# Attention and MLP kernel: batch 2 loaded six tokens to a partition, against odd batches that keep their first 64 tokens for the shared tile

## The chip, the cores and the metric

The kernel runs on one core of one Trainium2 chip. The metric is device time in microseconds (us), the median over runs of the whole program. Engines are named as in the profile: PE (TensorE) multiplies matrices, DVE is VectorE, ACT is ScalarE, POOL is GpSimd, SP is SyncE. POOL, SP and ACT can also issue DMAs.

## The reference, cut to what matters

```python
def _attn_ref(q, k, v, g_norm):                       # 8 batches, 8 heads, 576 tokens, 64 wide
    kv = np.einsum('bhsd,bhse->bhde', k, v)
    out = np.einsum('bhsd,bhde->bhse', q, kv)
    rms = np.sqrt(np.mean(out * out, axis=-1, keepdims=True) + 1e-06)
    return out / rms * g_norm

def _moe_ref(x, g_ln, w_ch1, w_ch2):                  # x: 8 x 576 x 512, heads side by side
    mu = np.mean(x, axis=-1, keepdims=True)
    var = np.mean((x - mu) ** 2, axis=-1, keepdims=True)
    xn = (x - mu) / np.sqrt(var + 1e-06) * g_ln
    ch = np.maximum(xn @ w_ch1, 0.0) @ w_ch2          # 512 -> 2048 -> 512
    return x + ch
```

Attention is linear: for each batch and head a 64 x 64 product of k and v over all tokens, which the queries are then multiplied by. Inputs and output are float32; the matrix products run in bf16.

## The kernel before

The 8 x 576 = 4608 rows of the output are 36 tiles of 128 rows (`TILES`, L81). A batch has 576 = 4 x 128 + 64 tokens: four tiles of its own, and a half. The halves of batches b and b+1 (b even) make one shared tile: tile 8 belongs to batches 0 and 1, 17 to 2 and 3, 26 to 4 and 5, 35, the last, to 6 and 7. Four tiles are a block of the MLP.

**Loads.** All input loads are DMAs issued by POOL, which cast float32 to bf16. POOL's queue is in order and holds eight DMAs at a time: the ninth waits for the first to land. Main loads of a batch put 4 neighbouring tokens on each of 128 partitions (slots 0 to 3); the remaining 64 tokens are loaded apart as a fifth slot (`load_fifth`, L269) on half of the partitions, and the other half of the slot is set to zero. Batches 0 and 1 load k and v with 6 tokens on each of 96 partitions (`load_kv`, L251), 96 x 6 = 576, so that they need no fifth slot; their queries have one as all do. `most` and `rest` (L64, L67) say which 64 tokens go apart: in even batches the last, in odd batches the first. So the rows of a shared tile, the end of one batch and the start of the next, are neighbours in the output and leave in one store (`tile_rows`, L76).

**One batch** (`plan_batch`, L727). For batches 0 to 2 ScalarE (for batch 0 VectorE) copies k from the landing buffer `kb` into `kp` with the heads innermost (`k_permute`, L411), and the queries from `qb` into `qp` (`q_permute`, L417); from batch 3 on the loads write that order themselves (`load_slots`, L282). `kv_mm` (L463) multiplies k by v on TensorE, heads in pairs: 24 matmuls over 96 rows for batches 0 and 1, 20 over 128 rows for the others. VectorE copies the result into `kv_pack` (L479). SP turns the queries with one DMA transpose for a batch (L449; batches 0 and 1 partly on TensorE, L427). From batch 3 on, POOL waits before each group of loads (`gate`, `gate_turn`) until a given earlier tile has been turned, or the queries of the batch before.

**One tile** (`plan_tile`, L822): output matmuls `out_ps` (L491), square on ScalarE (L517), sums (L526) and scaling on VectorE, centring (L579), then the turn of the centred tile into `xT`, on TensorE for the first 12 tiles (L586) with a copy by ScalarE (L593), by an SP DMA afterwards (L597).

**The MLP** (`plan_group`, L927). Up-projection: the first two blocks tile by tile, four groups of 16 matmuls each (`m1_fine`, L636), the others for a block at once (L651). ScalarE evicts each group with a ReLU (L643, L658). Down-projection: 16 matmuls a tile in four groups (L670); VectorE adds the residual (`y_out`, L677), and `store` (L681) writes the tile. Stores are issued by SP, except that the last tile is cut in three parts of 256, 128 and 128 columns, and the middle one is issued by ACT. Up- and down-projection groups share four PSUM banks (`BANKS["mm"]`).

**What sets the order.** Each step is entered with engine, estimated times, key and dependencies (`add`, L104). `run_plan` (L114) simulates the engines, picks for each the ready step with the lowest key within a short horizon, and the steps are emitted in the order of planned starts. Every engine then runs its instructions in that order. A step's `lag` makes the planner count its DMAs as later than estimated. So a changed load also moves matmuls and copies that it does not touch.

Of the kernel before, what the change touches and what calls it, by code (L numbers as in the profile page):

```python
# [14 lines left out]
def kernel(  # L15
# [11 lines left out]
    nc = tc.nc  # L27
# [6 lines left out]
    B, H, S, D = q.shape  # L34
# [15 lines left out]
    NEAR = 0.35  # L50
    BANKS = {"mm": 4, "out": 2, "kvt": 2}
    WARM_FROM = 1.3
    HALVED = (0,)
    SCALED = (0, 1)
    SPLIT_STORE = ()
    HALF_TURN = (0, 1)
    PARTS = ((0, 4), (4, 8))

# [1 line left out]

    def most(b):  # L64
        return slice(64 * (b % 2), 64 * (b % 2) + 512)

    def rest(b):  # L67
        return slice(0, 64) if b % 2 else slice(512, 576)

    def fifth(b):  # L70
        return slice(0, 64) if b % 2 == 0 else slice(64, 128)

    def no_fifth(b):
        return fifth(b + 1)

    def tile_rows(bs, t):  # L76

        return (bs[0] * S + most(bs[0]).start + t, 4) if t < 4 else (bs[0] * S + 512, 1)


    TILES = []  # L81
# [162 lines left out]
    kv_pack = [consts.tile([128, HP, 128], bf16, name=f"kv_pack{i}") for i in range(3)]  # L244

    def kv_view(buf, b):
        if b < 2:
            return buf[b % 2][0:96, :].rearrange("p (h t d) -> p h t d", h=H, t=6)
        return buf[b % 2][:, 0:H * 4 * D].rearrange("p (h t d) -> p h t d", h=H, t=4)

    def load_kv(buf, src, b, h0=0, h1=H):  # L251
        t = 6 if b < 2 else 4
        n = 576 if b < 2 else 512
        tokens = slice(0, 576) if b < 2 else most(b)
        def fn():
            nc.gpsimd.dma_start(  # L256
                kv_view(buf, b)[:, h0:h1, :, :].rearrange("p h t d -> p h (t d)"),
                src[b, h0:h1, tokens, :].rearrange("h (p t) d -> p h (t d)", t=t))
        return fn, n * (h1 - h0) * 256

    def load_q(b, t0, t1):
        def fn():
            nc.gpsimd.dma_start(
                qb[:, :, t0:t1, :].rearrange("p h t d -> p h (t d)"),
                q[b, :, most(b), :].rearrange("h (p t) d -> p h t d", t=4)[:, :, t0:t1, :]
                .rearrange("p h t d -> p h (t d)"))
        return fn, 128 * H * (t1 - t0) * 256

    def load_fifth(dst, src, b):  # L269
        def fn():  # L270
            nc.gpsimd.dma_start(
                dst[fifth(b), :, :], src[b, :, rest(b), :].rearrange("h p d -> p h d"))
        return fn, 64 * H * 256

    def load_slot(dst, src, b, t, h0=0, h1=H):
        def fn():
            nc.gpsimd.dma_start(  # L277
                dst[:, t, h0:h1, :],
                src[b, h0:h1, most(b), :].rearrange("h (p t) d -> p t h d", t=4)[:, t, :, :])
        return fn, 128 * (h1 - h0) * 256  # L280

    def load_slots(dst, src, b):  # L282
        def fn():
            nc.gpsimd.dma_start(
                dst[:, 0:4, :, :],
                src[b, :, most(b), :].rearrange("h (p t) d -> p t h d", t=4))
        return fn, 128 * H * 4 * 256


# [172 lines left out]

    def kv_mm(b, hps):  # L463
        ps = psum.tile([128, HP, 128], f32, tag="kvt", name="kv_ps", bufs=BANKS["kvt"])
        p, last = (slice(0, 96), 5) if b < 2 else (slice(0, 128), 4)
        for hp in hps:
            for t in range(last + 1):
                nc.tensor.matmul(  # L468
                    ps[:, hp, :],
                    lhsT=kp[b % 2][p, t, 2 * hp:2 * hp + 2, :].rearrange("p h d -> p (h d)"),  # L470
                    rhs=(v5[b % 2][:, 2 * hp:2 * hp + 2, :] if b >= 2 and t == 4
                         else kv_view(vb, b)[:, 2 * hp:2 * hp + 2, t, :]),
                    start=(t == 0), stop=(t == last))
            att[b]["kv", hp] = ps
# [203 lines left out]
            x[:, f0:f1], in0=st[n]["m2ps", f0], scalar=blk[m]["rstd"][:, i, :],  # L678
            in1=x[:, f0:f1], op0=ALU.mult, op1=ALU.add)

    def store(n, eng, f0=0, f1=Dm):  # L681
        r0, step = tile_rows(*TILES[n])
        eng.dma_start(out_flat[r0:r0 + 127 * step + 1:step, f0:f1], st[n]["x"][:, f0:f1])


    k0p = []
# [40 lines left out]
    def plan_batch(b):  # L727
# [23 lines left out]
        else:  # L751
# [9 lines left out]
                    pool_do(0.1, lambda: nc.gpsimd.tensor_copy(  # L761
                        mark, att[b - 1]["qT"][:, 0, 0:1]), [adone[b - 1]["qfree"]])
            dk = [adone[b - 2]["kvmm"]]
            if b < 4:

                pool_do(0.5, lambda: nc.gpsimd.memset(kp[b % 2][no_fifth(b), 4, :, :], 0.0), dk)
            gate(f - 8 if b > 3 else 5)
# [2 lines left out]
            if by_slot:  # L770
                pool_load(("k", b), load_slots(kp[b % 2], k, b), rate1, dk)
            else:
                pool_load(("k", b), load_kv(kb, k, b), rate4, dk)
            pool_load(("k", b), load_fifth(kp[b % 2][:, 4, :, :], k, b), 180.0, dk)
            def some_q():
                gate(f - 7 if b > 3 else 6)
                if by_slot:
# [24 lines left out]
            for t in range(5):  # L802
# [6 lines left out]
        s = add("PE", 1.12 if b > 1 else 1.34, 1.35 if b > 1 else 1.57, (p - 17.5 if b == 1 else ok - 4), vdeps + kperm,  # L809
                lambda: kv_mm(b, range(HP)), alloc="kvt")  # L810
        a = add("DVE", 0.34, 0.38, (p - 17 if b == 1 else ok - 2), [s, z1[4], z1[5]] + outs_before,
                lambda: kv_out(b, 0, HP, nc.vector, False))
# [114 lines left out]
    def plan_group(i, kind, a, c):  # L927
        if kind == "m1f":
            g = add("PE", 0.89, 1.1, i, done[a]["xT"] + load["w", 1, c], lambda: m1_fine(a, c),
                    alloc="mm", main=True)  # L930
            g.frees = add("ACT", *act_cost(512), i + 1, [g], lambda: m1_fine_out(a, c))
            done[a].setdefault("m1", []).append(g.frees)
            blk[a // 4]["m1done"] = g
        elif kind == "m1":
            g = add("PE", 0.864, 1.1, i, [d for j in range(4) for d in done[4 * a + j]["xT"]], lambda: m1_block(a, c),
                    alloc="mm", main=True)
            g.frees = add("ACT", *act_cost(512), i + 1, [g], lambda: m1_block_out(a, c))
            blk[a].setdefault("m1outs", []).append(g.frees)
            blk[a]["m1done"] = g
        else:  # L940
            n, m = a, a // 4
            m1s = done[n]["m1"] if m in FINE else blk[m]["m1outs"]
            split = n == N_TILES - 1
            parts = ((0, 256), (256, 384), (384, 512))
            if split:

                if c:
                    return
                for f0, f1 in parts:
                    w = (f1 - f0) / 256  # L950
# [12 lines left out]
            g = add("PE", 0.864, 1.1, i, m1s[:4 * (c + 1) if m not in FINE else 4] + load["w", 2, c],  # L963
                    lambda: m2(n, c), alloc="mm" if c == 0 else None, main=True)
            g.behind = done[n].get("last")
            done[n]["last"] = g
            if c == 0:
                done[n]["acc"] = g
            if c == 3:
                y = add("DVE", 0.66, 0.75, i + 2, [g, done[n]["rstd"]], lambda: y_out(n))  # L970
                done[n]["acc"].frees = y
                cols = ((0, 256), (256, 512)) if n in SPLIT_STORE else ((0, 512),)
                for f0, f1 in cols:
                    done[n]["store"] = add_dma(
                        "SP", i + 3, [y], lambda f0=f0, f1=f1: store(n, nc.sync, f0, f1),
                        262144 // len(cols), 340.0)
        mains_made.append(g)


# [79 lines left out]
```

## Time and profile before

| | |
|---|---|
| time, median of 3 runs | 293.06 us (292.58 to 293.21) |
| the profiled execution's own time | 293.06 us |
| its span | 291.3 us, 5178 instructions |
| granted TensorE clock | 1.0 throughout |
| PE busy | 283.6 us (97%) |
| DVE, ACT, POOL busy | 165.0, 142.6, 66.7 us |
| POOL's DMA queue (q0) | 18.35 MB, 66.0% of 16 engines |
| SP's DMA queue (q1) | 16.85 MB, 25.9% |
| TensorE's up- and down-projection groups | L636 30.6, L651 100.0, L670 128.1 us |
| k-by-v products (L468) | 168 matmuls, 11.0 us shown for 144 of them |

A busy time is a sum over the span; it does not say when. The chain that ended last follows the work back from the end, step by step, to what released each step. A group's line reads: line, engine, operation, output tile from input tiles, shape, count, then busy time, mean duration in ns, and the idle time before it with what ended that. Matmuls follow each other faster than one lasts (a 128-column matmul lasts 219 ns and the next starts after 56), so work on TensorE is costed by starts. In the DMA view a time to landing runs from the issue to the last increment of the DMA's semaphore.

### The profile page before, as it was taken

Reading aid. Unit: us, or ns where it says so; the run is one execution under the profiler, and the core shown is the slowest. Engines: PE = TensorE matmul, PEld = TensorE weight load, DVE = VectorE, ACT = ScalarE, POOL = GpSimd, SP = SyncE. Lnnn points to the kernel's source line nnn. Section 1 sums busy time; section 2 is a strip of 40 time slices with the busy share of each in tenths; the row PEclk is TensorE's granted clock in tenths of the full one; section 3 lists DMA queues with packets and bytes.
Section 4 is the critical chain, followed back from the end, with each engine's and each line's share of the span. In section 5 each row is a group of like instructions: output and inputs, shape, how many; then the busy total and the mean of one; then the engine's idle time right before and its main releaser. Section 6 shows DMA issues by size and latency. Waiting matters only on the chain.

```text
span 291.3 us, 5178 instructions
## 1 busy us (share of the span) xinstructions
PE 283.6 (97%) x2046; PEld 162.1 (56%) x2074; DVE 165.0 (57%) x362; ACT 142.6 (49%) x288; POOL 66.7 (23%) x93
## 2 busy tenths in 40 slices
PE   8899999999999999999999999999999999999995
PEld 6779845977645445444544445444544444444444
DVE  2696039487973997557755775477557755320022
ACT  2379954788756512761276126612761177017400
POOL 8974231007309006304060406000000000000000
PEclk9999999999999999999999999999999999999999
DMA  6999999948999998996999399922101210120012
GB/s 95 184 198 205 204 199 179 244 83 96 182 222 94 170 138 141 169 181 140 160 96 188 76 201 96 180 73 92 54 18 56 90 54 18 56 88 20 2 72 73
DMA packets 108332, 35.60 MB, mean 122 GB/s; under 512 B 87059, under 2 KB 103827, under 8 KB 108308
## 3 DMA queue, kind: packets, MB, share of 16 engines
q0 software_dynamic: 72624, 18.35, 66.0%
q1 hardware_dynamic: 35540, 16.85, 25.9%
q8 instruction: 16, 0.26, 0.4%
q14 instruction: 8, 0.07, 0.1%
q10 hardware_dynamic: 144, 0.07, 0.1%
HBM read 36.70 MB, written 9.44 MB: 158 GB/s over the span
## 4 chain that ended last, share of the span: by engine, by line
PE 85%; DMA 7%; POOL 6%; issue 1%; ACT 0%; DVE 0%; POOLq 0%
PE mm_ps L670 41%; PE mm_ps L651 33%; DMA qb<-in_q_dram 7%; PE mm_ps L636 5%; PE out_ps L491 3%; PE kv_ps L468 2%; POOL qp L277 1%; POOL w L361 1%; POOL vb L256 1%; POOL kb L256 1%; PE xT_ps L586 1%; POOL w L363 1%; PE qT_ps L427 0%; ACT qp L407 0%; POOL identity masks.py:197 0%
## 5 line engine op out<-in xcount | busy, mean ns | idle before, releaser
L670 PE MATMUL mm_ps<-w,m 128*128 128x512 bf16 (+2 forms) x592 | 128.1, 367 | 0.7
L651 PE MATMUL mm_ps<-xT,w 128*128 128x512 bf16 x436 | 100.0, 379 | 0.6
L658 ACT ACTIVATE m<-mm_ps 128x512 bf16<-128x512 f32 x112 | 66.8, 597 | 50.8 <-PE mm_ps L651 48.5
L670 PEld LDWEIGHTS <-m 128*128 128x128 bf16 x608 | 57.2, 98 | 60.6
L651 PEld LDWEIGHTS <-w 128*128 128x128 bf16 x448 | 43.1, 98 | 48.8
L526 DVE TENSOR_REDUCE ss<-sq 128x8 f32<-128x512 f32 (+1 forms) x37 | 24.8, 669 | 48.2 <-ACT sq L517 48.1
L677 DVE SCALAR_TENSOR_TENSOR x<-mm_ps,rstd,x 128x512 f32<-128x512 f32 (+2 forms) x38 | 27.3, 720 | 40.6 <-PE mm_ps L670 40.5
L517 ACT ACTIVATE sq<-out_ps 128x512 f32<-128x512 f32 (+1 forms) x37 | 21.6, 584 | 45.4 <-PE out_ps L491 45.4
L636 PE MATMUL mm_ps<-xT,w 128*128 128x128 bf16 x512 | 30.6, 219 | 0.0
L636 PEld LDWEIGHTS <-w 128*128 128x128 bf16 x512 | 29.2, 98 | 0.9 <-DMA w<-in_moe_w_ch_dram 0.2
L579 DVE SCALAR_TENSOR_TENSOR xc<-x,mv,gl 128x512 bf16<-128x512 f32 (+1 forms) x38 | 27.3, 723 | 1.2
L521 DVE TENSOR_TENSOR xg<-out_ps,gn 128x512 f32<-128x512 f32 x34 | 23.2, 683 | 0.2
L757 POOL COPY mark<-xT 128x1 bf16<-128x1 bf16 x15 | 7.5, 497 | 58.1 <-DMA xT<-xc 52.6
L643 ACT ACTIVATE m<-mm_ps 128x512 bf16<-128x512 f32 x32 | 18.4, 596 | 3.1 <-PE mm_ps L636 2.9
L530 ACT ACTIVATE rms<-ss,eps_attn 128x8 f32<-128x8 f32 (+1 forms) x37 | 11.1, 300 | 14.4 <-DVE ss L526 14.3
L557 DVE TENSOR_TENSOR x<-xg,inv 128x512 f32<-128x512 f32 x24 | 16.6, 692 | 0.8
L573 DVE BATCH_NORM_STATS2 stats<-x 128x6 f32<-128x512 f32 x24 | 16.6, 690 | 0.5
L491 PEld LDWEIGHTS <-qT 128*128 128x128 bf16 x160 | 11.4, 98 | 6.4 <-ACT qT L407 0.2
L491 PE MATMUL out_ps<-kv_pack,qT 128*128 128x128 bf16 x160 | 14.5, 219 | 0.2
L479 DVE CAST kv_pack<-kv_ps 64x256 bf16<-64x256 f32 x14 | 5.9, 422 | 11.9 <-PE kv_ps L468 11.8
L468 PEld LDWEIGHTS <-kp 128*128 128x128 bf16 (+1 forms) x168 | 10.5, 100 | 2.4 <-DMA vb<-in_v_dram 0.4
L468 PE MATMUL kv_ps<-vb,kp 128*128 128x128 bf16 (+1 forms) x144 | 11.0, 223 | 0.5 <-DMA vb<-in_v_dram 0.5
(69 smaller groups left out, 182.8 us busy)
## 6 DMA issues: line engine op xcount, KB each, us to landing
out_dram<-x SPq DMA_DIRECT2D x35, 256.0 KB, 2.5
w<-in_moe_w_ch_dram POOLq DMA_DIRECT2D x8, 512.0 KB, 12.3
vb<-in_v_dram POOLq DMA_DIRECT2D x6, 512.0 KB, 10.9
kp<-in_k_dram POOLq DMA_DIRECT2D x5, 512.0 KB, 9.5
qp<-in_q_dram POOLq DMA_DIRECT2D x5, 512.0 KB, 10.2
qb<-in_q_dram POOLq DMA_DIRECT2D x2, 512.0 KB, 18.1
qp<-in_q_dram POOLq DMA_DIRECT2D x10, 64.0 KB, 9.2
kb<-in_k_dram POOLq DMA_DIRECT2D x2, 288.0 KB, 5.6
```

The source lines that it names most:

```text
L468: nc.tensor.matmul(ps[:, hp, :], lhsT=kp[b % 2][p, t, 2 * hp:2 * hp + 2, :].rearrange("p h d -> p (h d)"), rhs=(v5[b % 2][:, 2 * hp:2 * hp ...
L491: nc.tensor.matmul(o3[:, hp, :], lhsT=att[b]["qT"][:, 4 * t + hp, :], rhs=kv_pack[b % 3][:, hp, :], start=(i == 0), stop=(i == len(bs) - 1))
L517: nc.scalar.activation(sq[:, h0:h1, :], st[n]["ps", h0][:, h0:h1, :], func=AF.Square)
L521: nc.vector.tensor_mul(xg[:, h0:h1, :], st[n]["ps", h0][:, h0:h1, :], gn.to_broadcast([128, h1 - h0, D]))
L526: nc.vector.tensor_reduce(ss[:, h0:h1, :], st[n]["sq"][:, h0:h1, :], axis=AX.X, op=ALU.add)
L579: nc.vector.scalar_tensor_tensor(xc[:, f0:f1], in0=st[n]["x"][:, f0:f1], scalar=blk[m]["mv"][:, i, 0:1], in1=gl[:, f0:f1], op0=ALU.subtrac ...
L636: nc.tensor.matmul(ps[:, d, :], lhsT=w1[c][:, kk, d * 128:(d + 1) * 128], rhs=blk[m]["xT"][:, kk, i * 128:(i + 1) * 128], start=(kk == 0), ...
L643: nc.scalar.activation(st[n]["m1"][:, c, :, :], st[n]["m1ps", c], func=AF.Relu)
L651: nc.tensor.matmul(ps, lhsT=w1[c][:, kk, d * 128:(d + 1) * 128], rhs=blk[m]["xT"][:, kk, :], start=(kk == 0), stop=(kk == nKm - 1))
L658: nc.scalar.activation(blk[m]["m1", c][:, d, :], blk[m]["m1ps", g], func=AF.Relu)
L670: nc.tensor.matmul(st[n]["m2ps", f0], lhsT=m1_piece(n, c, d), rhs=w2[c][:, d, f0:f1], start=(c == 0 and d == 0), stop=(c == 3 and d == 3))
L677: nc.vector.scalar_tensor_tensor(x[:, f0:f1], in0=st[n]["m2ps", f0], scalar=blk[m]["rstd"][:, i, :], in1=x[:, f0:f1], op0=ALU.mult, op1=AL ...
```

## The change

It replaces one treatment of the 64 odd tokens by another, in four parts.

1. Batch 2 joins batches 0 and 1 (`SIXES = 3`): k and v in 6 tokens on each of 96 partitions, no fifth-slot load for either, 24 matmuls. Its k is copied in four pieces of two heads instead of two of four. The `lag` of its copies is 3 instead of 4, and the key of the copies moves. The memsets of the empty half of k's fifth slot move from batches 2 and 3 to batches 3 and 4.
2. All batches keep their first 512 tokens in slots 0 to 3 and the last 64 for the fifth; `most` and `rest` go.
3. A shared tile's rows are no longer neighbours in the output, so each shared tile is stored in two halves of 64 rows. In the last tile SP stores batch 6's half and ACT batch 7's, of each of the three parts.
4. The stores of tiles 23 and 25 are split in two by columns.

In the emitted order this makes two DMAs less on POOL (57 in place of 59), six more on SP and two more on ACT, and two copies more on ACT. Batch 2's k-by-v product moves from behind tile 4's first down-projection group to the place ahead of tile 5's first up-projection group, its query copies ahead of tile 5's evictions, and batch 3's product 16 matmuls forward.

```diff
+    SIXES = 3
...
-    SPLIT_STORE = ()
+    SPLIT_STORE = (23, 25)
...
-    def most(b):
-        return slice(64 * (b % 2), 64 * (b % 2) + 512)
-    def rest(b):
-        return slice(0, 64) if b % 2 else slice(512, 576)
...
-    def tile_rows(bs, t):
-        return (bs[0] * S + most(bs[0]).start + t, 4) if t < 4 else (bs[0] * S + 512, 1)
+    def tile_rows(b, t):
+        if t < 4:
+            return [(slice(0, 128), b * S + t, 4, 128)]
+        return [(fifth(b), b * S + 512, 1, 64)]
...
     def load_kv(buf, src, b, h0=0, h1=H):
-        t = 6 if b < 2 else 4
-        n = 576 if b < 2 else 512
-        tokens = slice(0, 576) if b < 2 else most(b)
+        t = 6 if b < SIXES else 4
+        n = 576 if b < SIXES else 512
...
     def kv_mm(b, hps):
-        p, last = (slice(0, 96), 5) if b < 2 else (slice(0, 128), 4)
+        p, last = (slice(0, 96), 5) if b < SIXES else (slice(0, 128), 4)
...
-    def store(n, eng, f0=0, f1=Dm):
-        r0, step = tile_rows(*TILES[n])
-        eng.dma_start(out_flat[r0:r0 + 127 * step + 1:step, f0:f1], st[n]["x"][:, f0:f1])
+    def store(n, b, eng, f0=0, f1=Dm):
+        for p, r0, step, num in tile_rows(b, TILES[n][1]):
+            eng.dma_start(
+                out_flat[r0:r0 + (num - 1) * step + 1:step, f0:f1], st[n]["x"][p, f0:f1])
...
-            if b < 4:
+            if b in (SIXES, SIXES + 1):
                 pool_do(0.5, lambda: nc.gpsimd.memset(kp[b % 2][no_fifth(b), 4, :, :], 0.0), dk)
...
-                pool_load(("k", b), load_kv(kb, k, b), rate4, dk)
-            pool_load(("k", b), load_fifth(kp[b % 2][:, 4, :, :], k, b), 180.0, dk)
+                pool_load(("k", b), load_kv(kb, k, b), rate6, dk)
+            if b >= SIXES:
+                pool_load(("k", b), load_fifth(kp[b % 2][:, 4, :, :], k, b), 180.0, dk)
...
-                pool_load(("v", b), load_fifth(v5[b % 2], v, b), 100.0, dk)
+                if b >= SIXES:
+                    pool_load(("v", b), load_fifth(v5[b % 2], v, b), 100.0, dk)
...
-            for h0, h1 in ((0, 4), (4, 8))[by_slot * 2:]:
-                kperm.append(add("ACT", 0.85, 1.0, ok - 16, load["k", b][0:1] + dk,
-                                 lambda h0=h0, h1=h1: k_permute(nc.scalar, b, h0, h1)))
+            for h0 in () if by_slot else (0, 2, 4, 6):
+                kperm.append(add("ACT", 0.63, 0.75, ok - 13, load["k", b][0:1] + dk,
+                                 lambda h0=h0: k_permute(nc.scalar, b, h0, h0 + 2)))
...
-                x.lag = 4.0 if b == 2 else 6.0
+                x.lag = 3.0 if b == 2 else 6.0
...
-                    if 0 < f0 and f1 < Dm:
-                        add("ACT", 0.55, 2.3, i + 3, [y], lambda f0=f0, f1=f1: store(
-                            n, nc.scalar, f0, f1))
-                    else:
-                        add_dma("SP", i + 3, [y], lambda f0=f0, f1=f1: store(
-                            n, nc.sync, f0, f1), 131072 * w, 300.0)
+                    for e, b in zip((nc.sync, nc.scalar), TILES[n][0]):
+                        if e is nc.sync:
+                            add_dma("SP", i + 3, [y], lambda f0=f0, f1=f1, b=b: store(
+                                n, b, nc.sync, f0, f1), 65536 * w, 300.0)
+                        else:
+                            add("ACT", 0.55, 2.3, i + 3, [y], lambda f0=f0, f1=f1, b=b: store(
+                                n, b, nc.scalar, f0, f1))
...
-                cols = ((0, 256), (256, 512)) if n in SPLIT_STORE else ((0, 512),)
-                for f0, f1 in cols:
+                for b in TILES[n][0]:
+                    cols = ((0, 256), (256, 512)) if n in SPLIT_STORE else ((0, 512),)
+                    for f0, f1 in cols:
```

More of the change, by code (lines that the diff above doesn't have):

```diff
@@ L246, in kv_view @@
     def kv_view(buf, b):
-        if b < 2:
+        if b < SIXES:
             return buf[b % 2][0:96, :].rearrange("p (h t d) -> p h t d", h=H, t=6)
@@ L257, in fn @@
                 kv_view(buf, b)[:, h0:h1, :, :].rearrange("p h t d -> p h (t d)"),
-                src[b, h0:h1, tokens, :].rearrange("h (p t) d -> p h (t d)", t=t))
+                src[b, h0:h1, 0:n, :].rearrange("h (p t) d -> p h (t d)", t=t))
         return fn, n * (h1 - h0) * 256
@@ L264, in fn @@
                 qb[:, :, t0:t1, :].rearrange("p h t d -> p h (t d)"),
-                q[b, :, most(b), :].rearrange("h (p t) d -> p h t d", t=4)[:, :, t0:t1, :]
+                q[b, :, 0:512, :].rearrange("h (p t) d -> p h t d", t=4)[:, :, t0:t1, :]
                 .rearrange("p h t d -> p h (t d)"))
@@ L271, in fn @@
             nc.gpsimd.dma_start(
-                dst[fifth(b), :, :], src[b, :, rest(b), :].rearrange("h p d -> p h d"))
+                dst[fifth(b), :, :], src[b, :, 512:576, :].rearrange("h p d -> p h d"))
         return fn, 64 * H * 256
@@ L278, in fn @@
                 dst[:, t, h0:h1, :],
-                src[b, h0:h1, most(b), :].rearrange("h (p t) d -> p t h d", t=4)[:, t, :, :])
+                src[b, h0:h1, 0:512, :].rearrange("h (p t) d -> p t h d", t=4)[:, t, :, :])
         return fn, 128 * (h1 - h0) * 256
@@ L285, in fn @@
                 dst[:, 0:4, :, :],
-                src[b, :, most(b), :].rearrange("h (p t) d -> p t h d", t=4))
+                src[b, :, 0:512, :].rearrange("h (p t) d -> p t h d", t=4))
         return fn, 128 * H * 4 * 256
@@ L470, in kv_mm @@
                     lhsT=kp[b % 2][p, t, 2 * hp:2 * hp + 2, :].rearrange("p h d -> p (h d)"),
-                    rhs=(v5[b % 2][:, 2 * hp:2 * hp + 2, :] if b >= 2 and t == 4
+                    rhs=(v5[b % 2][:, 2 * hp:2 * hp + 2, :] if b >= SIXES and t == 4
                          else kv_view(vb, b)[:, 2 * hp:2 * hp + 2, t, :]),
@@ L808, in plan_batch @@
         outs_before = adone[b - 3].get("outs", []) if b >= 3 else []
-        s = add("PE", 1.12 if b > 1 else 1.34, 1.35 if b > 1 else 1.57, (p - 17.5 if b == 1 else ok - 4), vdeps + kperm,
+        s = add("PE", 1.12 if b >= SIXES else 1.34, 1.35 if b >= SIXES else 1.57, (p - 17.5 if b == 1 else ok - 4), vdeps + kperm,
                 lambda: kv_mm(b, range(HP)), alloc="kvt")
@@ L971, in plan_group @@
                 done[n]["acc"].frees = y
-                cols = ((0, 256), (256, 512)) if n in SPLIT_STORE else ((0, 512),)
-                for f0, f1 in cols:
-                    done[n]["store"] = add_dma(
-                        "SP", i + 3, [y], lambda f0=f0, f1=f1: store(n, nc.sync, f0, f1),
-                        262144 // len(cols), 340.0)
+                for b in TILES[n][0]:
+                    cols = ((0, 256), (256, 512)) if n in SPLIT_STORE else ((0, 512),)
+                    for f0, f1 in cols:
+                        done[n]["store"] = add_dma(
+                            "SP", i + 3, [y], lambda b=b, f0=f0, f1=f1: store(n, b, nc.sync, f0, f1),
+                            262144 // len(TILES[n][0]) // len(cols), 340.0)
         mains_made.append(g)
```

## The prediction

> **What bounds the kernel now.** The page comes first: its busy times, then the chain that ended last.
>
> ```profile
> PE 283.6 (97%) x2046; PEld 162.1 (56%) x2074; DVE 165.0 (57%) x362; ACT 142.6 (49%) x288; POOL 66.7 (23%) x93
> ...
> PE 85%; DMA 7%; POOL 6%; issue 1%; ACT 0%; DVE 0%; POOLq 0%
> ```
>
> TensorE is busy for 97% of the span and carries 85% of the chain; the DMA and POOL shares are the start, before about 39 us. The waits of TensorE, asked for from 18 us to the end, show how tight that is: one wait.
>
> ```profile
> PE qT_ps L427 <- ACT qp L407: 0.3, 1, 0.3
> ```
>
> So nothing that only makes another engine or a DMA faster can gain time after 18 us. What counts is how much TensorE is given, whether the new order makes it wait, and what follows its last matmul. That end is in the timeline of the last microseconds (columns: start, duration, engine, line, tile) and in the DMA view from 288.2 to 290.5.
>
> ```profile
> 284.82 3.04 PE L670 MATMUL mm_ps<-w,m 128*128 128x256 bf16 x42
> ...
> 287.39 0.37 ACTq L683 DMA_DIRECT2D out_dram<-x  x1
> 287.90 0.35 DVE L677 SCALAR_TENSOR_TENSOR x<-mm_ps,rstd,x 128x128 f32<-128x128 f32 x1 [0.54 <-PE mm_ps L670]
> ```
>
> ```profile
> q14 instruction: 1, 0.01, 1.6%
> issues: line engine op xcount, KB each, median us to landing
> out_dram<-x SPq DMA_DIRECT2D x1, 64.0 KB, 2.1
> ```
>
> TensorE stops at 287.9, VectorE finishes the last 128 columns at 288.25, SP issues their store at 288.28, it lands 2.06 us later (290.34), and closing code takes the span to 291.27. The whole run is 293.06 us, the median of the three shown, so 1.8 us lie outside the span. In that last store 15 of 16 semaphore increments came by 289.83 and one at 290.34; the instruction packet in the same window held one DMA engine for 1.6% of 16 x 2.3 us, 0.59 us.
>
> Last, where the change bites: TensorE's and ScalarE's timelines around batch 2, and POOL's issues.
>
> ```profile
> 53.17 0.61 PE L491 MATMUL out_ps<-kv_pack,qT 128*128 128x128 bf16 x8
> 53.62 4.63 PE L636 MATMUL mm_ps<-xT,w 128*128 128x128 bf16 x80
> 58.09 1.03 PE L670 MATMUL mm_ps<-w,m 128*128 128x512 bf16 x3
> 58.95 0.39 PE L468 MATMUL kv_ps<-vb,kp 128*128 128x128 bf16 x4
> ```
>
> ```profile
> 48.76 1.98 ACT L407 COPY kp<-kb 128x1024 bf16<-128x1024 bf16 x2
> 51.59 0.58 ACT L593 COPY xT<-xT_ps 128x512 bf16<-128x512 bf16 x1 [0.85 <-PE xT_ps L586]
> ...
> 59.87 1.99 ACT L407 COPY qp<-qb 128x1024 bf16<-128x1024 bf16 x2
> ```
>
> ```profile
> 30.90 0.88 POOL L256 DMA_DIRECT2D kb<-in_k_dram  x1 [1.64 <-DMA kb<-in_k_dram]
> 33.78 0.68 POOL L271 DMA_DIRECT2D kp<-in_k_dram  x1 [1.99 <-DMA vb<-in_v_dram]
> 36.30 0.88 POOL L256 DMA_DIRECT2D vb<-in_v_dram  x1 [1.84 <-DMA w<-in_moe_w_ch_dram]
> 39.56 0.69 POOL L271 DMA_DIRECT2D v<-in_v_dram  x1 [2.38 <-DMA qb<-in_q_dram]
> 42.24 0.88 POOL L263 DMA_DIRECT2D qb<-in_q_dram  x1 [1.99 <-ACT qT L407]
> ```
>
> With their times to landing (17.4, 16.0, 15.8, 14.0, 16.7 us) these five land at 48.3, 49.8, 52.1, 53.6 and 58.9: one backlog, served in order.
>
> **TensorE's work.** Batch 2's k-by-v product goes from 20 matmuls over 128 rows to 24 over 96. Batch 1 already has that form: its 24 matmuls run from 34.12 to 35.46, 1.34 us; batch 2's 20 take 58.95 to 60.07, 1.12 us. **+0.22 us**, all on the path. No other matmul is added.
>
> **The loads of batch 2.** The two 64 KB tails of k and v go (1.5 us each between the landings above), and the two main loads grow from 512 to 576 KB. Batch 1's two 576 KB loads land at 30.6 and 33.5, 2.9 us apart; batch 2's v landed 2.3 us behind the k tail. So k lands at 48.3 + 0.6 = 48.9, v at 48.9 + 2.9 = 51.8. The queries landed 5.3 us behind the v tail while four output stores shared the engines: at worst 51.8 + 5.3 = 57.1, at best, ahead of those stores, 51.8 + 2.9 = 54.7. I take 55, near the best: the trace has their first packets at 51.2, 2.4 us ahead of the v tail's landing, so they would start at about 49.4, and the stores' first packet comes at 51.9. No gain by itself: TensorE was not waiting.
>
> **Does the new order wait?** The instruction order puts the product one group after 53.17 and moves the output matmuls of tiles 6 and 7 behind it. In TensorE's terms: one group of 16 (0.89) ends at 54.07, the product (1.34) at 55.41, the two tiles (0.45) at 55.86, tile 5's four groups (3.57) at 59.43.
> - Product at 54.07: v is there at 51.8. The k copies become four of 96x768. Rows: 1.47 us for 96x1536, 1.04 for 128x1024, which is 0.85 ns an element, so 0.82 each and 0.72 from start to start. From 48.9 they end at 51.9, against 50.74 now. 2.2 us to spare. The xT copy behind them starts at about 51.8 instead of 51.59; its reader is at 55.86.
> - ScalarE, in its new order: square of tile 6 from 55.8 (0.6), a small root (0.2), then both query copies, from 56.6 for 1.9 us, and only then tile 5's first eviction, 58.5 to 59.1. TensorE needs that PSUM bank at 59.43. **0.3 us of cover**: this is the thinnest place. If the queries land after 56.9, every microsecond later is a microsecond of stalled TensorE, because the evictions stand behind the copies in ScalarE's queue.
> - The query copies end 3.3 us earlier than now (58.5 for 61.8), so batch 2's transpose on SP, POOL's gate behind it (66.96 now) and batch 3's loads move 3.3 us earlier too. Batch 3's product is moved ahead by 16 matmuls of 0.216, 3.45 us, to about 85.7; its v tail landed at 84.0 and comes at 80.7. 5 us to spare. Tile 9's output matmuls stand at 65.3, the transpose lands at 63.6.
> I take no wait: **0**.
>
> **SP's and POOL's queues.** Six more stores on SP (three shared tiles in two halves, two tiles split by columns, one in the last tile), 0.38 us each, 2.3 us over the run. SP waited 83 us for VectorE's results in 31 waits, so these hide in that; if they did not, the xT transposes behind them would be 0.38 us late, at places where TensorE's next reader is blocks away. POOL loses two issues of 0.7 us and keeps two memsets of 0.52 us, now for batches 3 and 4, in front of gates where it idles for microseconds. The shifted rows of odd batches move no bytes differently. 0.
>
> **The end.** The last tile's three stores become two each, half on SP and half on ACT. The last pair is issued 0.22 us later, at 288.50, both engines free (0.38 and 0.40 us an issue, evacuations 0.9 apart). How long to landing no row shows for 64 rows of 512 B. Rows near it: ACT's 64 KB, 1.6 us; SP's 64 KB, 1.55 without the engine that fetched instructions, 2.06 with it. Half the bytes on each queue cannot need more than the same bytes on one, unless the queues obstruct each other. I take 1.6: SP has seven more instructions ahead of its end, so a fetch tied to a place in its stream should come several instructions earlier. Landing 290.10 instead of 290.34, **-0.24 us with the 0.22 in it**. Bounds: 1.27, ACT's 1.6 less all of the 0.33 us in which its packets ran (-0.57), and 2.46, SP's 2.06 and one issue of 0.40 in line (+0.62).
>
> The Trainium skill ("DMA: Bandwidth & Descriptors", section "Rules for kernel authors") speaks against the split: spreading DMAs over SP, ACT and GpSimd does not help bandwidth, since all run on the same 16 engines. By that rule alone the last store would cost what it does now, and the sum would be 293.28. It also says ("Runtime: NRT & Kernel Launch", section "Instruction fetch mechanics") that a fetch is mostly hidden; the increment 0.5 us behind the other fifteen says otherwise here.
>
> **Sum:** 293.06 - 0.24 = 292.82, that is +0.22 for TensorE and -0.46 for a last landing of 1.6 instead of 2.06.
>
> **Rivals.**
> - Faster: the last pair, 32 KB each, lands in 1.27 us. For: half the packets for each queue, no fetch. Against: SP's 128 KB store took 1.7 and ACT's 64 KB 1.6, so size matters little. 293.06 - 0.57 = 292.49. Chance 0.25.
> - Slower, one mechanism: the queries land late and hold ScalarE's queue. It decides from 56.9 on. If they land where they do now, 58.9, TensorE loses 2.0 us at tile 4's first down-projection: 294.8. Against: two tails less in front of them. Chance 0.1.
> - Slower at the end: the fetch falls on the last pair again, or the two queues obstruct each other: landing 2.46, 293.06 + 0.62 = 293.68. Chance 0.2.
> - The change does not do what it says: the query tail is still loaded, so "no fifth slot" is true of k and v only; the order shows exactly two loads less, so I give this no chance of its own.
>
> **How the numbers follow.** The forecast has 0.45, with a range of its own from 292.6 to 293.3 (landings of 1.4 to 2.06). The line is 0.2% (0.59 us, about what a measurement of this kernel can tell from no change), so 292.47 and 293.65; the three runs of before lie 0.63 apart, so each case is smeared by some 0.3. Faster: most of the fast end and a tenth of the forecast, 0.2. Slower: both slow cases but a tenth of them, 0.27. Within: 0.53. The range 292.3 to 294.0 reaches over the fast and the slow end, smear included, and leaves out the late queries.
>
> **What would show it.** Right: 24 matmuls of batch 2's product from about 54.1 without a wait before them; query copies from about 56.6; no wait of TensorE for ScalarE near 59.4; TensorE's end at 288.1; last stores of 32 KB landing in 1.6 us. Wrong: an idle of TensorE before the down-projection near 59.4 (late queries), before the product (late v), or a last landing over 2 us.

## The result, and the profile after

The changed kernel takes 294.98 us (median of 6, 294.77 to 295.97) against 292.94 for the kernel before, run on the same chip: a ratio of 1.0072 with a 95% interval from 1.0053 to 1.009. It is slower by 2.0 us, beyond the range of the prediction. The profiled execution took 295.12 us, its span is 293.3, so 1.8 us lie outside the span as before. The first lines to read are those of the page that the prediction began with, busy times and chain:

```profile
PE 283.6 (97%) x2050; PEld 162.6 (55%) x2078; DVE 165.1 (56%) x362; ACT 143.3 (49%) x290; POOL 66.3 (23%) x91
...
PE 74%; DMA 18%; POOL 3%; DVE 2%; ACT 2%; issue 1%; POOLq 0%
```

TensorE's share of the chain fell from 85% to 74% and the DMAs' rose from 7% to 18%. The waits of TensorE from 18 us on, a single one of 0.3 before, are now three:

```profile
PE mm_ps L664 <- ACT m L637: 0.8, 1, 0.8
PE out_ps L485 <- DMA qT<-qp: 0.7, 1, 0.7
PE out_ps L485 <- ACT qT L401: 0.3, 1, 0.3
```

The third lies at 18.1 us, in the start, which the loads set. The first two are new, and TensorE's timeline shows where they sit (start, duration, line, tile, and the idle time before it with what ended that):

```profile
54.07 1.51 PE L462 MATMUL kv_ps<-vb,kp 96*128 96x128 bf16 x24
55.41 0.61 PE L485 MATMUL out_ps<-kv_pack,qT 128*128 128x128 bf16 x8
55.86 3.74 PE L630 MATMUL mm_ps<-xT,w 128*128 128x128 bf16 x64
60.36 1.02 PE L664 MATMUL mm_ps<-w,m 128*128 128x512 bf16 x3 [0.76 <-ACT m L637]
...
67.10 0.40 PE L485 MATMUL out_ps<-kv_pack,qT 128*128 128x128 bf16 x4 [0.67 <-DMA qT<-qp]
```

The k-by-v product stands at 54.07 with nothing idle ahead of it and takes 1.34 us to the next start, 0.22 more than before. Tile 5's 64 matmuls start at 55.86 and need 3.57 by their starts, so tile 4's down-projection should start at 59.43; it starts at 60.36, 0.93 late (the page shows 0.76, since it counts idle time from the modelled end of a matmul). From 60.36 to tile 9's output matmuls is 5.91 us of work, 66.27; they start at 67.10, 0.83 late. ScalarE and POOL say why:

```profile
48.77 3.02 ACT L401 COPY kp<-kb 96x768 bf16<-96x768 bf16 x4
51.69 0.58 ACT L587 COPY xT<-xT_ps 128x512 bf16<-128x512 bf16 x1
...
57.82 1.99 ACT L401 COPY qp<-qb 128x1024 bf16<-128x1024 bf16 x2 [1.20 <-DMA qb<-in_q_dram]
59.72 0.59 ACT L637 ACTIVATE m<-mm_ps 128x512 bf16<-128x512 f32 x1
```

```profile
34.27 0.77 POOL L250 DMA_DIRECT2D vb<-in_v_dram  x1 [2.26 <-PE mm_ps L630]
41.23 0.88 POOL L257 DMA_DIRECT2D qb<-in_q_dram  x1 [6.18 <-ACT qp L401]
```

The queries' load lands 16.6 us after its issue at 41.23, at 57.8. ScalarE stands idle 1.2 us for it, then copies for 1.9, and only then evicts the bank that TensorE waits for. TensorE ends 2.00 us later than before: its last result is scaled by VectorE from 289.90 instead of 287.90. 0.22 + 0.93 + 0.83 = 1.98 of that is named. From VectorE's end (290.25) to the end of the span it takes 3.06 us, before 3.02: the tail brought nothing. Its DMAs, from 288.2 us to the end (KB each, median time to landing):

```profile
out_dram<-x SPq DMA_DIRECT2D x1, 64.0 KB, 1.9
out_dram<-x ACTq DMA_DIRECT2D x1, 64.0 KB, 2.2
out_dram<-x SPq DMA_DIRECT2D x2, 32.0 KB, 1.8
out_dram<-x ACTq DMA_DIRECT2D x2, 32.0 KB, 2.1
```

### The profile page after: what moved, and what is told of

It is laid out like the page before. It is cut to its first block, busy times and chain, and to the rows that moved or that the text cites. A ratio compares the mean times of both kernels' runs of the same rounds, so it can differ in the third digit from the quotient of the medians.

```text
span 293.3 us, 5200 instructions
## 1 busy us (share of the span) xinstructions
PE 283.6 (97%) x2050; PEld 162.6 (55%) x2078; DVE 165.1 (56%) x362; ACT 143.3 (49%) x290; POOL 66.3 (23%) x91
## 3 DMA queue, kind: packets, MB, share of 16 engines
q0 software_dynamic: 71056, 18.35, 63.6%
## 4 chain that ended last, share of the span: by engine, by line
PE 74%; DMA 18%; POOL 3%; DVE 2%; ACT 2%; issue 1%; POOLq 0%
PE mm_ps L664 35%; PE mm_ps L645 32%; DMA qb<-in_q_dram 12%; DMA w<-in_moe_w_ch_dram 3%; PE out_ps L485 3%; DMA qT<-qp 2%; PE kv_ps L462 2%; PE mm_ps L630 2%; ACT qp L401 1%; POOL qp L271 1%; POOL vb L250 1%; DVE x L671 1%; POOL kb L250 1%; PE xT_ps L580 0%; POOL w L355 0%
## 5 line engine op out<-in xcount | busy, mean ns | idle before, releaser
L752 POOL COPY mark<-xT 128x1 bf16<-128x1 bf16 x15 | 9.0, 600 | 57.9 <-DMA xT<-xc 53.5
L551 DVE TENSOR_TENSOR x<-xg,inv 128x512 f32<-128x512 f32 x24 | 16.6, 692 | 0.8
L567 DVE BATCH_NORM_STATS2 stats<-x 128x6 f32<-128x512 f32 x24 | 16.6, 690 | 0.5
L462 PE MATMUL kv_ps<-vb,kp 128*128 128x128 bf16 (+1 forms) x152 | 11.6, 226 | 0.6 <-DMA vb<-in_v_dram 0.5
```

Source lines behind the costliest of these rows:

```text
L462: nc.tensor.matmul(ps[:, hp, :], lhsT=kp[b % 2][p, t, 2 * hp:2 * hp + 2, :].rearrange("p h d -> p (h d)"), rhs=(v5[b % 2][:, 2 * hp:2 * hp ...
```

## The experiments

Ten kernels ran, each in several rounds beside the kernel before, whose median was 293.05 to 293.12 us in these comparisons.

**Which part of the change.** First the change without part 1: batch 2 loaded and copied as before, all else as changed.

```diff
-    SIXES = 3
+    SIXES = 2
...
-            for h0 in () if by_slot else (0, 2, 4, 6):
-                kperm.append(add("ACT", 0.63, 0.75, ok - 13, load["k", b][0:1] + dk,
+            for h0 in () if by_slot else (0, 4):
+                kperm.append(add("ACT", 0.85, 1.0, ok - 16, load["k", b][0:1] + dk,
...
-                x.lag = 3.0 if b == 2 else 6.0
+                x.lag = 4.0 if b == 2 else 6.0
```

> Edit: the changed kernel with batch 2 treated as before (4 tokens to a partition, fifth slots, two copies of k): what is left of the change is the halved stores of the shared tiles, the two split stores and the last tile's six half stores on SP and ACT. TensorE's, VectorE's and POOL's orders are those of the kernel before. Theory now: the last pair, issued at once on two queues, lands 2.0 us after its issue as in the changed kernel (1.80 and 2.05), against 2.06 before: 292.9. Rival, the prediction's own step: the landing is 1.6 and the time 292.94 - 0.46 = 292.5; the 2.05 of the changed kernel would then be a chance of one execution. Rival: six more stores on SP cost TensorE a wait: 293.3 and more.

293.18 us, ratio 0.9998 [0.9975, 1.0021]: rows, stores and tail together cost and bring nothing that this comparison can tell (its interval is some 0.6 us to either side). TensorE has no wait of its own from 18 us on, so the further stores on SP are hidden, as predicted. Then part 1 alone, on the kernel before (the first pair of lines stands for the like edits of `kv_view`, `load_kv`, `kv_mm`, the fifth slots and their memsets):

```diff
-        if b < 2:
+        if b < 3:
...
-            for h0, h1 in ((0, 4), (4, 8))[by_slot * 2:]:
+            for h0, h1 in () if by_slot else ((0, 2), (2, 4), (4, 6), (6, 8)):
...
-                x.lag = 4.0 if b == 2 else 6.0
+                x.lag = 3.0 if b == 2 else 6.0
```

> Edit: the kernel before with part 1 of the change alone (batch 2 six to a partition, k copied in four pieces, lag 3); stores as before. TensorE's, VectorE's, ScalarE's and POOL's orders up to the last tile are those of the changed kernel. Theory: the whole loss is in this part, 0.22 of work, 0.93 and 0.83 of waits: 292.94 + 1.98 = 294.9, with a last store of 64 KB on SP as before. Rival: the waits come in part from the stores (the shared tile 8's two half stores and their packets between 50 and 60 us): then one of the two waits is smaller, 293.9 to 294.4.

294.61 us, 1.004 [1.0017, 1.0064]; the profiled execution 294.82. The loss is in part 1: 1.5 us of the 2.0 by the medians, clear of noise. Its waits differ from the changed kernel's, though. The only one from 18 us on, and the chain:

```profile
PE mm_ps L670 <- ACT m L643: 2.1, 1, 2.1
```

```profile
40.94 17.92 DMA qb<-in_q_dram
58.88 1.99 ACT qp L407 x2
```

Here the queries landed at 58.9, one microsecond later than in the changed kernel's profile, and all the waiting is in one place, at 61.42. By then the transpose was in time for tile 9. So the first wait varies with the landing, and the second depends on the first, which moves the reader.

**Why the queries land late, and whether their landing decides.** Four stores of 256 KB (tiles 0 to 3) are issued from 48.2 to 51.9 in both kernels; their first packets come at 51.95 before and 52.12 after. The queries' packets, 512 bytes each, start at 49.75 in the changed kernel and at 51.18 in the kernel before. The next kernel moves the stores behind the transpose in SP's order.

```diff
     order = run_plan()
+    late = [done[n]["store"] for n in range(4)]
+    order = [s for s in order if s not in late]
+    at = order.index(adone[2]["qfree"]) + 1
+    order[at:at] = late
```

> Edit: the changed kernel with the stores of tiles 0 to 3 (four of 256 KB, issued between 48.2 and 51.9, their increments at 53.9 to 60.2) put behind batch 2's query transpose in SP's order; every other engine's order is that of the changed kernel. Theory: these stores share the DMA engines with the queries' load and are why it lands at 57.8 and not near 55. Without them it lands at 54.7 to 55.5 (2.9 us behind v at 52.3, as one such load needed at 30.6 to 33.5), the copies stand at 56.6 to 58.5, both waits of TensorE go: 294.98 - 1.76 = 293.2, unless the stores, now beside the transpose, make that late. Rival: the small packets of batch 1's transposes, or the queue as such, hold the load up: landing 57 or later, and the wait at 59.4 stays: 294.1 or more.

293.59 us, 1.0016 [0.9998, 1.0034]; profiled 293.18. The queries land at 55.4, ScalarE copies from 56.38, and TensorE waits neither at 59.29 nor at 65.20:

```profile
55.72 3.74 PE L630 MATMUL mm_ps<-xT,w 128*128 128x128 bf16 x64
59.29 1.03 PE L664 MATMUL mm_ps<-w,m 128*128 128x512 bf16 x4
...
63.42 1.95 PE L630 MATMUL mm_ps<-xT,w 128*128 128x128 bf16 x32
65.20 0.39 PE L485 MATMUL out_ps<-kv_pack,qT 128*128 128x128 bf16 x4
```

With the stores in that place the whole load lands at 57.8 to 58.9 (five profiles), without them at 55.4. But two things have left the window: SP's queue is in order, so batch 1's second query transpose now goes 7.4 us earlier too (44.62 in place of 52.06). The DMA view from 52 to 55.8 us tells which of them counts (packets, MB, their time as a share of 16 engines), first in the changed kernel, then in this one:

```profile
q1 hardware_dynamic: 473, 0.88, 67.4%
q0 software_dynamic: 778, 0.27, 60.1%
```

```profile
q0 software_dynamic: 1271, 0.44, 99.3%
q1 hardware_dynamic: 227, 0.05, 11.7%
```

In the changed kernel the transpose's packets (256 bytes) begin at 55.81, when 979 of the queries' 1024 packets have started. Up to then SP's queue q1 carries the stores alone, and the loads' queue q0 moves 0.27 MB where it moves 0.44 without them. So the stores are the cause of most of the delay; whether the transpose adds to its end is not separated.

In the next, `load_q` brings half of batch 2's queries (the source is cut likewise).

```diff
-                qb[:, :, t0:t1, :].rearrange("p h t d -> p h (t d)"),
+                qb[:, :, t0:t0 + (2 if b == 2 else t1 - t0), :].rearrange("p h t d -> p h (t d)"),
```

> Leaves out half of batch 2's queries: their load brings slots 0 and 1 only (256 KB instead of 512), the planner being told of all, so that every order is the changed kernel's. Theory: the landing decides the first wait, above a threshold of 56.9; half of the 5.5 us between v's landing (52.3) and the queries' (57.8) saved puts it at 55.0: no wait at 59.4, the transpose is issued at about 58.6 and its reader at 65.3 waits at most for the one increment that came late: 293.2 to 293.5. Rival: the copies' place in ScalarE's order costs by itself, whenever the queries land: 294 or more.

293.47 us, 1.0009 [0.999, 1.0029]. Landing at 55.3, copies from 56.53, the down-projection at 59.44 without a wait; tile 9's output matmuls stand at 65.59, 0.23 late, behind the transpose's last increment at 65.55. Same order on every engine, an earlier landing, no loss at the evictions: the copies' place costs nothing by itself. The other way round, the landing left as it is and the copies moved:

```diff
-                x.lag = 3.0 if b == 2 else 6.0
+                x.lag = (8.0 if x in qperm else 3.0) if b == 2 else 6.0
```

> Edit: the planner counts batch 2's queries as landing 8 us late instead of 3 for their copies alone; in the emitted order both query copies go behind tile 5's four evictions, and tiles 9 and 10's output matmuls to about 70.1. Loads as in the changed kernel. Theory: both waits (0.93 for tile 5's evictions behind the copies, 0.83 for the transpose) come from where the order put the copies and their readers, with queries landing at 57.8: both gone, 0.22 of the 1.98 us left, 294.98 - 1.76 = 293.2. Rival: what is late is the load itself, and the wait only moves to the transpose's new reader at 70.1 or to batch 3's loads behind POOL's gate: 294 to 295.

293.37 us, 1.0005 [0.9985, 1.0025]. The queries land at 57.9, no earlier than in the changed kernel, the copies run behind tile 5's evictions, tile 9's output matmuls stand at 70.08, and TensorE waits for none of it:

```profile
59.34 1.03 PE L664 MATMUL mm_ps<-w,m 128*128 128x512 bf16 x3
...
61.56 1.99 ACT L401 COPY qp<-qb 128x1024 bf16<-128x1024 bf16 x2
```

What is left is the 0.22 us of work, too little for the comparison to tell from nothing.

**The second wait.** In the changed kernel 15 of the 16 increments of the query transpose came by 65.49 and one at 67.05. First its reader was moved back:

```diff
-            turn.lag = 5.0 if by_slot else 0.0
+            turn.lag = 5.0 if by_slot else 3.0 if b == 2 else 0.0
```

> Edit: the planner counts batch 2's query transpose as landing 3 us later; in the emitted order tile 9's output matmuls go 16 matmuls (0.89 us of TensorE) further back, all else up to there as in the changed kernel. Theory: 0.83 us of the loss is TensorE waiting at 66.27 for the transpose, whose 16th increment came at 67.05 (the other 15 by 65.49). With its reader at 66.2 + 0.93 = 67.1 that wait is gone and nothing takes its place: 294.98 - 0.83 = 294.15; the wait of 0.93 at 59.43 stays. Rival: tile 9 is needed early, and the same 0.8 us comes back at a later reader of tile 9 (its transpose, block 2's first matmul): 294.98.

294.85 us, 1.0048 [1.0027, 1.0068]: inconclusive as a time. In the profiled execution the granted clock was below full in the first 30 us (0.86 from 10 to 20 us, 0.97 from 20 to 30), which put TensorE 1.3 us behind at the product; its mean clock was 0.994, as in six more of the twelve, and the executions at full clock spread from 294.08 to 295.77. Its trace is of use all the same. SP issued the four stores 1.3 us later too, at 49.6, the queries landed at 56.2, in line with the runs above, and TensorE waits for nothing from 18 us on. Of the transpose, 15 increments came by 64.90 and one at 66.45. In both traces an instruction packet of TensorE, 16384 bytes, lies in the transpose's last microsecond, at 65.05 (0.95 us long) and at 64.44 (0.93). The DMA view of the changed kernel from 64 to 67.2 us has it:

```profile
q8 instruction: 1, 0.02, 1.8%
```

To move it, TensorE's stream was made shorter:

```diff
-            elif gap > 0.3 and not s.main and (s not in urgent or gap > 0.45):
+            elif gap > 30.0 and not s.main and (s not in urgent or gap > 0.45):
```

> Edit: the changed kernel without the 51 idle matmuls that fill TensorE's gaps between 8.8 and 18 us; all else, and every other engine, in the same order. TensorE's stream is 102 instructions shorter there, so its instruction packet at 65.05 (0.95 us, in the last microsecond of the query transpose) comes some 2.8 us later, at 67 to 68. Theory: that packet held the one DMA engine whose increment came at 67.05 while 15 came by 65.49 (the same in three other runs with a packet at 62.9 to 64.4); moved away, all 16 increments come within 0.2 us and the wait before tile 9's output matmuls goes, the one at 59.4 stays: 294.98 - 0.83 = 294.15, if the clock in the first 20 us stays at 1.0 without the filling. Rival: the late increment is the transpose's own: still one 1.5 us behind the rest.

295.47 us, 1.008 [1.0067, 1.0093]; the expected 294.15 missed, since the queries landed at 58.8 and the first wait grew. The packet came at 68.07, and the transpose's increments all lie between 65.53 and 65.68. TensorE's timeline:

```profile
61.35 1.02 PE L664 MATMUL mm_ps<-w,m 128*128 128x512 bf16 x4 [1.87 <-ACT m L637]
...
67.26 0.39 PE L485 MATMUL out_ps<-kv_pack,qT 128*128 128x128 bf16 x4
```

No wait at tile 9. That alone would prove little, since the longer first wait moved the reader to 67.26; the increments do. The packet also made another DMA late at its new place: of the store that SP issued at 67.24, 15 increments came by 69.65 and one at 70.95, while all 16 of its counterpart in the changed kernel lie between 68.17 and 68.53. Four traces with such a packet starting 0.3 to 0.5 us before the transpose's other increments have one increment 1.5 to 1.6 us late (the changed kernel, and the runs with the turn later, half the queries and the stores later); with it at 68.07, or at 61 in the kernel before, there is none. With a packet at 65.30 in the run of part 1 alone, 0.3 to 0.5 us before the increments (65.62 to 65.77), there was none either. The moment was the same there, so the moment is not enough; which DMA engine a packet is on the traces do not tell.

**The tail.** First part 1 on the old stores, with the copies behind the evictions, that is part 1 alone as above and:

```diff
-                x.lag = 3.0 if b == 2 else 6.0
+                x.lag = (8.0 if x in qperm else 3.0) if b == 2 else 6.0
```

> Edit: part 1 of the change alone on the kernel before (rows and stores as before), with the query copies behind tile 5's evictions as in the run with later copies (293.37). Theory: the last tile's pair on two queues costs 0.45 us against one 64 KB store without an instruction fetch in it (2.05 against 1.6 in the run with part 1 alone), and the fetch at the end comes when ScalarE reaches about its 319th instruction, which part 1's two more copies move from 289 to 277 us: 293.37 - 0.45 = 292.9. Rival: the split costs nothing, the last landing stays over 2 us: 293.4.

292.98 us, 1.0002 [0.9987, 1.0017]. The same order with the new stores had 1.0005 [0.9985, 1.0025], so the times cannot tell the two tails apart. In the trace the last 64 KB landed in 1.6 us. Then the kernel before, with four tiny ScalarE instructions more:

```diff
-    nc.scalar.activation(warm, eps_ln, func=AF.Sqrt)
+    for _ in range(5): nc.scalar.activation(warm, eps_ln, func=AF.Sqrt)
```

> Edit: the kernel before with four tiny ScalarE instructions more at its start (the first activation, 128x1, 0.2 us, five times in place of once, in the 2.2 us in which ScalarE waits for TensorE). Nothing else moves. Theory: the instruction packet that delays the last store is ScalarE's and comes with about its 319th instruction; four instructions more bring it to about 273 us, the last store lands in 1.6 instead of 2.06: 0.45 below the kernel before, some 292.5. Rival, the prediction's reading: the packet belongs to a place in SP's stream, which does not move: no difference from the kernel before.

292.61 us against 293.12, ratio 0.9983 [0.9969, 0.9998]: faster than the kernel before, by an interval that ends just short of 1. The profiled executions lie 0.8 us apart, 0.3 of it ahead of VectorE's end and 0.5 behind it. The view of its last 4 us has no instruction packet any more, and the last line, 2.1 before, is 1.6:

```profile
q1 hardware_dynamic: 288, 0.20, 14.7%
q10 hardware_dynamic: 144, 0.07, 5.5%
issues: line engine op xcount, KB each, median us to landing
out_dram<-x SPq DMA_DIRECT2D x1, 128.0 KB, 1.7
out_dram<-x ACTq DMA_DIRECT2D x1, 64.0 KB, 1.6
out_dram<-x SPq DMA_DIRECT2D x1, 64.0 KB, 1.6
```

The packet went from 289.0 to 247.3 us, and two more moved forward (34.2 to 32.2, 144.9 to 133.8); those at 163.6 and 190.7 stayed (164.0 and 191.0 before). Only ScalarE's stream got longer, so those that moved are ScalarE's. I had expected it at 273; which instruction calls it is open. Last, the split alone on top of this:

```diff
-                    if 0 < f0 and f1 < Dm:
-                        add("ACT", 0.55, 2.3, i + 3, [y], lambda f0=f0, f1=f1: store(
-                            n, nc.scalar, f0, f1))
-                    else:
-                        add_dma("SP", i + 3, [y], lambda f0=f0, f1=f1: store(
-                            n, nc.sync, f0, f1), 131072 * w, 300.0)
+                    add_dma("SP", i + 3, [y], lambda f0=f0, f1=f1: store(
+                        n, nc.sync, f0, f1, 0, 64), 65536 * w, 300.0)
+                    add("ACT", 0.55, 2.3, i + 3, [y], lambda f0=f0, f1=f1: store(
+                        n, nc.scalar, f0, f1, 64, 128))
```

> Edit: the kernel before with the four tiny ScalarE instructions (292.61, last store 64 KB on SP landing in 1.6 us), and its last tile's three stores cut into halves of 64 rows on SP and ACT as in the change. Theory: two queues that issue at once lengthen each other's way: last landing 2.05 to 2.1 instead of 1.6, 292.61 + 0.45 = 293.05. Rival: the pair is as good as the one store and the 2.05 of the changed kernel came from its other edits: 292.6.

293.91 us, 1.0032 [1.0015, 1.005]; profiled 293.29, so the median lies above what was expected. The profiled execution is 1.0 us longer than that of the run before: 0.2 ahead of VectorE's end, 0.5 from there to the last landing, and 0.4 in the closing code, 1.30 us behind the last landing in place of 0.93, which nothing here explains. The term itself is plain:

```profile
out_dram<-x SPq DMA_DIRECT2D x2, 32.0 KB, 1.8
out_dram<-x ACTq DMA_DIRECT2D x2, 32.0 KB, 2.1
```

From VectorE's end to the last landing it is 2.07 us, 1.59 without the split: 0.48 for the split. It changes two things at once, the number of queues and the shape of a store (64 rows), and no run has one without the other at the end. The changed kernel's trace has a hint from earlier. Tile 26's two halves of 64 rows (issued at 231.00 and 231.55) and tile 25's two halves by columns (227.67 and 228.05) all leave on SP, 128 KB each; the DMA view has the pair by rows first, then the pair by columns:

```profile
out_dram<-x SPq DMA_DIRECT2D x2, 128.0 KB, 2.3
```

```profile
out_dram<-x SPq DMA_DIRECT2D x2, 128.0 KB, 1.9
```

The issues took 506 and 582 ns by rows, 333 and 424 by columns, and the first packet of the first half came 1.16 us after its issue by rows, 0.83 by columns. So with a single queue at work the shape of 64 rows already goes with a longer issue, a later start and a later landing. How much of the 0.48 the second queue adds stays open.

## Why the prediction was wrong

**The step that failed first** is a term of "The loads of batch 2": "I take 55, near the best", with 57.1 as the worst. The measured landings are 57.8, 58.8 and 58.9, and in place of "no wait: 0" TensorE lost 0.93 us for it in the changed kernel and 0.83 at tile 9. The best end put the load ahead of the stores. That was not to be had: the stores are issued at 48.2 to 51.9 in the trace of before too, and the queries' packets start only 1.4 us earlier than they did (49.75 for 51.18). Starting earlier moved the load deeper into the same four stores, and it came out where it had, 0 to 1.1 us earlier. The worst end took 5.3 us behind v's landing as a fixed time, but that time was set by when the stores were done (their increments run to 58.7 before), not by where the load began. Of the 0.7 us by which even 57.1 fell short, 0.5 is v's landing, 52.3 for 51.8.

**The mechanism was right**, and named as the slow rival with its threshold and price: copies ahead of tile 5's evictions in ScalarE's queue, cover 0.3 us, a microsecond of stall for each microsecond after 56.9, 294.8 for a landing at 58.9. In three traces TensorE resumes 2.56 us after the landing (57.80 and 60.36, 58.86 and 61.42, 58.79 and 61.35), and part 1 alone with its 58.9 took 294.82 in the profiled execution. That this meets 294.8 within 0.02 is luck in part: by its starts the wait there is 2.28 us (59.14 to 61.42), not 2.0, and other terms make up for it. The rival deserved far more than its chance of 0.1: the same load landed at 58.9 in the only trace there was.

**Tile 9.** "Stand at 65.3, the transpose lands at 63.6" took 5 us from issue to landing. Fifteen increments needed 5.1 (60.40 to 65.49); the sixteenth needed 6.66, late with TensorE's instruction packet beside it and in time where the packet had been moved away. The change had made this wait possible: it moved the reader forward, in front of a landing that before had room.

**The end.** "I take 1.6" was 2.05. The sentence that half the bytes on each queue cannot need more than all on one "unless the queues obstruct each other" left room for the answer in its last clause: the split cost 0.48 us when it was made alone, though how much of it by two queues and how much by stores of 64 rows is open. In the changed kernel the issue took 469 to 486 ns on SP and 501 to 641 on ACT in place of 332 and 369, and the first packets of the 128-column parts came 1.14 and 1.40 us after the issue in place of 0.84 and 0.87. The instruction packet did leave the last store, as forecast, but not for the reason given: it belongs to ScalarE, not to SP. So -0.50 and +0.49 cancelled. The Trainium skill's "DMA: Bandwidth & Descriptors", section "Rules for kernel authors", also advises one 128-partition transfer over two to disjoint halves of the partitions, because both use the same engines; these runs agree with the advice and add a price, 0.48 us at the end of this kernel; its reason no run here tests. By the rule that the prediction quoted from that page the tail would have been worth nothing, and that is the net result, but by two terms that happen to cancel.

**What held:** the 0.22 us (1.34 for 24 matmuls); the product at 54.07 without a wait; the k copies at 0.72 to 0.73 us apart and the xT copy at 51.69 for 51.8; batch 3's product without a wait; nothing from SP's further stores or POOL's queue.

## What to carry to other kernels

When a transfer is issued earlier, look at what shares the DMA engines in its new window before giving it the gain: a landing set by other traffic does not move with the issue. Where an in-order engine has copies for such a landing ahead of evictions, cost the order by the latest landing that the traces show, or put the evictions first (that alone took 1.6 us off here, by the medians). And look at what delays the very last store, increment by increment: half a microsecond lay behind an instruction packet that four tiny instructions moved away.

## What the runs showed of the hardware

Instruction packets take part in the traffic: one of 16384 bytes for TensorE (0.9 to 3.0 us beside loads and stores) or of 8192 bytes for another engine (0.3 to 0.8 us) goes with one of a DMA's 16 increments coming late, by 1.3 to 1.6 us for TensorE's and by 0.5 for ScalarE's in the kernel before, where that DMA is near its end (the transposes and the stores above). The Trainium skill ("Runtime: NRT & Kernel Launch", section "Instruction fetch mechanics") calls the cost of such a fetch mostly hidden. For TensorE itself the trace of the kernel before agrees, 15 such packets from 18 us on and one wait, 0.3 us for a copy; for a transfer that another engine waits for it does not hold here.

Without the 51 idle matmuls in TensorE's gaps the granted clock fell to 0.66 between 10 and 20 us in the profile, and its mean to 0.983 to 0.986 in three of four executions. With them it was 1.0 in that stretch in the profiles of all kernels here but the one with the turn later, which has them all and still fell to 0.86. So they seem to help, and do not settle it.
